# Moving the first LayerNorm of blocks 1 to 3 to earlier steps of a fused attention and feed-forward kernel

## The chip, the cores and the metric

The kernel runs on one core of one Trainium2 chip. The metric is the device time of one execution in microseconds, lower being better.

## The reference, cut to what matters

One adaptive-LayerNorm block: attention over the last 512 cached keys, then a feed-forward part, both with a residual. Shapes: x is 2048 x 512, 32 query heads of 128, 8 key heads.

```python
def _layernorm(x, axis=-1, eps=1e-05):
    m = jnp.mean(x, axis=axis, keepdims=True)
    v = jnp.var(x, axis=axis, keepdims=True)
    return (x - m) / jnp.sqrt(v + eps)
# ... sa, ca, ga, sb, cb, gb are the six 512-wide rows of silu(c) @ w_mod
x = A_x
h = _layernorm(x, axis=-1) * (1 + ca) + sa
x = x + ga * _A_ref(h, A_k_cache, A_v_cache, A_wq, A_wo)     # attention
h = _layernorm(x, axis=-1) * (1 + cb) + sb
x = x + gb * _B_ref(h, B_w1, B_w2)                           # feed-forward
```

There are two LayerNorms per row: "the first" feeds the Q projection, "the second" feeds the feed-forward part.

## The kernel before

The 2048 queries are four blocks of 512. The program is written as 128 steps, one head of one block each (32 steps per block), and a feed-forward tail. In each step TensorE gets scores, the Q projection of a later step, the PV product (softmax weights times values) of the step before, and up to four output-projection matmuls. All other work is a *task* with a step at which it is put into its engine's instruction stream; in the VectorE lines of the prediction, the reciprocal behind a write that stands 3.83 us comes only after it, so a late task holds up what is behind it.

```python
def add_ln(b, which, s0):
    dst, r = (hT[b % 2], R_hT[b % 2]) if which == 1 else h2_of[b]
    for tl in range(TPB):
        add(s0 + tl, lambda t=b * TPB + tl: ln_stat(t))                  # steps s0 .. s0+3
    add(s0 + TPB, lambda: ln_rstd(b))                                    # s0+4
    for tl in range(TPB):
        add(s0 + TPB + 1 + tl // 2, lambda t=b * TPB + tl: ln_norm(t))   # s0+5, s0+6: writes xn
    add(s0 + TPB + 2, ln_dmaT)                                           # s0+6: DMA transpose xn -> xnT
    for cc in range(DC):
        add(s0 + TPB + 5 + cc // 2, lambda cc=cc: ln_mod_sb(cc, dst, r, which))   # s0+9, s0+10: reads xnT
```

There is one `xn` and one `xnT` tile, used by every LayerNorm. `ln_norm` and `ln_mod_sb` (the scale-and-shift that makes hT for Q and h2T for the feed-forward) run on VectorE. VectorE also empties the single buffer in PSUM, the memory that matmuls write into, of the PV product, and the next PV product waits for that:

```python
def pv_mms(u):
    # ... 16 matmuls into o_ps
    kb.op(DVE, lambda e: e.reciprocal(rinv[:, u, :], o_ps[:, :, P]), ...)        # L1511
    kb.op(DVE, lambda e: e.tensor_tensor(o_sb[u % NOS][:, :, :], o_ps[...], rinv[...], op=ALU.mult), ...)   # L1512
    dma(oT[u % NOT][:, :, :], o_sb[u % NOS][:, :, :]..., transpose=True)
```

## Time and profile before

| | before |
|---|---|
| median (first three runs) | 563.0 us (562.78 to 563.45) |
| profiled span | 561.0 us |
| TensorE busy / VectorE busy | 98% / 45% |
| PV beat, with / without output projection | 3.497 / 2.633 us |
| PV intervals off the beat among the first 126 | 8, together 1.33 us too long |

The most useful reading of this kernel is not a busy share but the *beat*: the list of times at which each of the 128 PV products starts, taken from the TensorE timeline. Each interval should be 2.633 or 3.497 us; whatever is longer is time that TensorE lost. The profile lines are in the prediction below.

### The profile page before, as it was taken

To read this page: it belongs to the slowest core of one execution; us is meant where nothing else is said; L and a number is where in the kernel's file an instruction comes from. 1 tells how busy PE (TensorE), PEld (TensorE's weight loads), DVE (VectorE), ACT (ScalarE), POOL (GpSimd) and SP (SyncE) were. 2 spreads that over 40 slices of the span, in tenths; PEclk is the share of its full clock that TensorE was granted. 3 is DMA by queue.
4 is the path that set the end of the run, shared out by engine and by line. 5 is a ranking of instruction groups with operands and counts; after the bars stand their busy time and mean duration, and the time that the engine had idled before them with its cause. 6 is when DMAs were issued, how large, how long until landed. Compare 5 with 4: busy or idle time off the path is not lost.

```text
span 561.0 us, 9655 instructions
## 1 busy us (share of the span) xinstructions
PE 550.8 (98%) x4057; PEld 314.7 (56%) x4132; DVE 252.4 (45%) x550; ACT 350.4 (62%) x453; POOL 51.7 (9%) x46
## 2 busy tenths in 40 slices
PE   7999999999999999999999999999999999999998
PEld 3565555555555555555555555555555654444444
DVE  3455556643336745333347453333354448321134
ACT  5986666666666666666666666666666644432500
POOL 1020002003220000033000000332000000000000
PEclk9999999999999999999999999999999999999999
DMA  9797566512132155242532531121214210210001
GB/s 270 205 206 176 143 164 88 113 39 38 39 76 39 39 90 136 56 96 57 132 57 57 85 63 39 39 38 39 39 39 72 44 30 0 40 37 23 21 29 47
DMA packets 113308, 42.66 MB, mean 76 GB/s; under 512 B 93928, under 2 KB 112104, under 8 KB 113256
## 3 DMA queue, kind: packets, MB, share of 16 engines
q1 hardware_dynamic: 112024, 40.82, 34.5%
q10 hardware_dynamic: 1232, 1.15, 0.6%
q8 instruction: 33, 0.54, 0.4%
q14 instruction: 19, 0.16, 0.1%
HBM read 18.35 MB, written 2.10 MB: 36 GB/s over the span
## 4 chain that ended last, share of the span: by engine, by line
PE 93%; DMA 4%; DVE 2%; issue 1%; DVEq 0%
PE psS L1367 27%; PE psO L1367 26%; PE psQ L1367 22%; PE psW L1367 18%; DMA xnT<-xn 3%; DMA x<-in_A_x_dram 1%; DVE o L1512 0%; DVE st L1377 0%; DVE xn L1388 0%; PE psS L1370 0%; DVE acc L1534 0%; DVE mv L1378 0%; DVE hT L1396 0%; DVE rinv L1511 0%; DVE rstd L1593 0%
## 5 line engine op out<-in xcount | busy, mean ns | idle before, releaser
L1501 ACT ACTIVATE PT<-psS 128x1024 bf16<-128x1024 f32 x256 | 262.7, 1028 | 128.2 <-PE psS L1367 128.2
L1367 PE MATMUL psS<-qT,kT 128*128 128x512 bf16 x510 | 151.4, 379 | 0.1
L1367 PEld LDWEIGHTS psO<-v,PT 128*128 128x128 bf16 x2048 | 126.3, 98 | 31.9 <-DVE o L1512 2.6
L1367 PE MATMUL psO<-v,PT 128*128 128x129 bf16 x2048 | 137.0, 220 | 0.6 <-DVE o L1512 0.6
L1367 PE MATMUL psQ<-hT,wq 128*128 128x512 bf16 x505 | 130.2, 379 | 0.2
L1367 PE MATMUL psW<-wo,oT 128*128 128x512 bf16 x452 | 118.1, 379 | 3.2
L1511 DVE RECIPROCAL rinv<-psO 128x4 f32<-128x4 f32 x128 | 23.3, 182 | 216.0 <-PE psO L1367 216.0
L1512 DVE TENSOR_TENSOR o<-psO,rinv 128x512 bf16<-128x512 f32 x128 | 88.5, 691 | 4.7 <-DVE rinv L1511 0.3
L1367 PEld LDWEIGHTS psQ<-hT,wq 128*128 128x128 bf16 x508 | 49.6, 98 | 60.7 <-issue 0.5
L1367 PEld LDWEIGHTS psS<-qT,kT 128*128 128x128 bf16 x512 | 49.5, 98 | 58.9 <-ACT PT L1501 0.7
L1493 ACT ACTIVATE qT<-psQ 128x512 bf16<-128x512 f32 x127 | 75.3, 593 | 0.5 <-PE psQ L1367 0.5
L1680 ACT ACTIVATE wq<-psS 128x512 bf16<-128x512 f32 x56 | 33.4, 597 | 49.4 <-PE psS L1367 49.4
L1367 PEld LDWEIGHTS psW<-wo,oT 128*128 128x128 bf16 x512 | 44.9, 98 | 32.9 <-DVE acc L1534 1.2
L1534 DVE TENSOR_TENSOR acc<-psW,acc 128x512 f32<-128x512 f32 x48 | 33.1, 690 | 6.7 <-PE psW L1367 6.7
L1367 PE MATMUL psO<-wmw,wq 128*128 128x512 bf16 (+1 forms) x164 | 32.7, 352 | 0.3
L1537 POOL TENSOR_TENSOR acc<-acc,gaf 128x512 f32<-128x512 f32 x12 | 15.2, 1266 | 156.5 <-DVE acc L1534 149.7
L1383 POOL TENSOR_TENSOR rstd<-rstd,cst 128x4 f32<-128x4 f32 x7 | 7.2, 1033 | 213.5 <-DVE rstd L1382 213.5
L1691 DVE TENSOR_TENSOR PT<-psO,gbf 128x512 f32<-128x512 f32 (+1 forms) x12 | 7.5, 624 | 40.4 <-PE psO L1367 40.4
L1367 PE MATMUL psS<-h2T,wmw 128*128 128x512 bf16 x110 | 25.2, 379 | 0.1
L1367 PEld LDWEIGHTS psO<-wmw,wq 128*128 128x128 bf16 x168 | 15.3, 98 | 16.6
L1367 PE MATMUL psS<-hT,wmw 128*128 128x512 bf16 x110 | 24.4, 379 | 0.1
L1377 DVE BATCH_NORM_STATS2 st<-x 128x6 f32<-128x512 bf16 x31 | 21.0, 678 | 4.7 <-DMA x<-in_A_x_dram 4.7
(77 smaller groups left out, 189.4 us busy)
## 6 DMA issues: line engine op xcount, KB each, us to landing
wo<-in_A_wo_dram SPq DMA_DIRECT2D x4, 1024.0 KB, 6.0
wq<-in_A_wq_dram SPq DMA_DIRECT2D x7, 512.0 KB, 5.7
wmw<-in_B_w_dram SPq DMA_DIRECT2D x14, 256.0 KB, 3.1
wmw<-in_w_mod_dram SPq DMA_DIRECT2D x5, 512.0 KB, 4.8
oT<-o SPq DMA_TRANSPOSE x128, 2.4
out_dram<-PT SPq DMA_DIRECT2D x15, 128.0 KB, 1.7
x<-in_A_x_dram SPq DMA_DIRECT2D x3, 512.0 KB, 4.2
v<-in_A_v_cache_dram SPq DMA_DIRECT2D x8, 128.0 KB, 4.2
```

The lines of the kernel that those rows point to most:

```text
L1367: kb.op(PE, lambda e: e.matmul(out_ap, lhsT, rhs, start=start, stop=stop), reads=reads, group_writes=[R_b[k] for k in bk], signal=signal)
L1377: kb.op(DVE, lambda e: e.bn_stats(st[:, t, :], x_sb[:, t, :]), reads=[R_x[t]], writes=[R_st[t]])
L1383: kb.op(POOL, lambda e: e.tensor_tensor(rstd[:, sl], rstd[:, sl], cst[:, 0:1].to_broadcast([P, hi - lo]), op=ALU.pow), reads=R_rstd[sl] + ...
L1493: kb.op(ACT, lambda e: e.activation(qT[u % NQT][:, :], bank[bk], ACTF.Copy), reads=[R_b[bk]], writes=[R_qT[u % NQT]])
L1501: kb.op(ACT, lambda e: e.activation(PT[u % NPT][:, pr * 2:pr * 2 + 2, :], s_ps[pr][:, :, :], ACTF.Exp, scale=scale), reads=[R_b[pr * 2], R ...
L1511: kb.op(DVE, lambda e: e.reciprocal(rinv[:, u, :], o_ps[:, :, P]), reads=[R_b[5], R_b[6]], writes=[R_rinv])
L1512: kb.op(DVE, lambda e: e.tensor_tensor(o_sb[u % NOS][:, :, :], o_ps[:, :, 0:P], rinv[:, u, :].unsqueeze(2).to_broadcast([P, TPB, P]), op=A ...
L1534: kb.op(DVE, lambda e: e.tensor_tensor(acc[:, tl, :], bank[WBK], acc[:, tl, :], op=ALU.add), reads=[R_b[WBK], R_acc[tl]], writes=[R_acc[tl]])
L1537: kb.op(eng, lambda e: e.tensor_tensor(acc[:, tl, :], acc[:, tl, :], gaf[:, :], op=ALU.mult), reads=[R_acc[tl], R_ga], writes=[R_acc[tl]])
L1680: kb.op(ACT, lambda e: e.activation(h1T[b % 2][:, fc, :], bank[bk], ACTF.Relu), reads=[R_b[bk]], writes=[R_h1[b % 2][fc]], pre=all_events( ...
L1691: kb.op(DVE, lambda e: e.tensor_tensor(yt[i][:, c0:c1], bank[bk][:, c0:c1], gbf[:, c0:c1], op=ALU.mult), reads=[R_b[bk], R_gb], writes=[R_ ...
```

## The change

Its effect: the first LayerNorm of a block is never under way in the same steps as the second LayerNorm of another block. The diff moves it nine steps (from 15 to 24 steps ahead of the block), its x load ten, and rearranges the modulation sums and the value-range reductions of the first 38 steps to make room for block 1.

```diff
-            add(max(R * g, 3), lambda g=g, i=i, op=op: kb.op(DVE, lambda e: e.tensor_reduce(vmax...
+            add((3, 5, 12, 16, 20, 24, 28, 32)[g], lambda g=g, i=i, op=op: kb.op(DVE, lambda e: e.tensor_reduce(vmax...
 ...
     for b in range(1, NB):
-        add(H * b - 20, lambda b=b: load_x(b))
-        add_ln(b, 1, H * b - 15)
+        add(H * b - 30, lambda b=b: load_x(b))
+        add_ln(b, 1, H * b - 24)
     for b in range(NB - 1):
         add_ln(b, 2, H * (b + 1) + 19)
 ...
-    for sl, steps in ((2, (5, 6, 7, 9)), (3, (10, 11, 13, 14)), (4, (15, 25, 26, 27)), (5, (29, 30, 31, 33))):
+    for sl, steps in ((2, (6, 7, 15, 19)), (3, (21, 22, 23, 25)), (4, (26, 27, 29, 30)), (5, (31, 33, 34, 35))):
 ...
-    for sl, s in ((2, 10), (3, 27), (4, 38), (5, 105)):
+    for sl, s in ((2, 20), (3, 27), (4, 36), (5, 105)):
```

More of the change, by code (lines that the diff above doesn't have):

```diff
@@ L1634, in build_fast @@
         for i, op in enumerate((ALU.max, ALU.min)):
-            add(max(R * g, 3), lambda g=g, i=i, op=op: kb.op(DVE, lambda e: e.tensor_reduce(vmax[:, i, g:g + 1], v_sb[:, g, :, 0:Dh], axis=AX.XY, op=op),
+            add((3, 5, 12, 16, 20, 24, 28, 32)[g], lambda g=g, i=i, op=op: kb.op(DVE, lambda e: e.tensor_reduce(vmax[:, i, g:g + 1], v_sb[:, g, :, 0:Dh], axis=AX.XY, op=op),
                                                              reads=[R_v[g]], writes=[R_vmax]))
```

## The prediction

> **What bounds the kernel now.** I read the page first, then the waits of all engines, then the timelines of TensorE and VectorE around the places that the waits name.
>
> ```profile
> PE 550.8 (98%) x4057; PEld 314.7 (56%) x4132; DVE 252.4 (45%) x550; ACT 350.4 (62%) x453; POOL 51.7 (9%) x46
> PE   7999999999999999999999999999999999999998
> PE 93%; DMA 4%; DVE 2%; issue 1%; DVEq 0%
> ```
>
> TensorE is the bound from the second slice to the end; nothing else is close. The whole question is therefore how many microseconds TensorE stands still because of the work that the change moves. The kernel runs in 128 steps (one head of one block of 512 queries each), then a feed-forward tail. In a step, TensorE does scores, a Q projection, the PV product and, when there is work, four output-projection matmuls. I listed the start of every PV product from the PE timeline: with output projection the beat is 3.497 us, without it (the first eight intervals and two near the end) 2.633 us, and it repeats to 1 ns in 118 of the first 126 intervals. Only in two places is it off. This is the PE timeline at the first of them:
>
> ```profile
> 202.37 1.07 PE L1367 MATMUL psO<-v,PT 128*128 128x129 bf16 x16
> ...
> 206.33 1.08 PE L1367 MATMUL psO<-v,PT 128*128 128x129 bf16 x16 [0.30 <-DVE o L1512]
> ...
> 209.84 1.07 PE L1367 MATMUL psO<-v,PT 128*128 128x129 bf16 x16
> ...
> 213.51 1.08 PE L1367 MATMUL psO<-v,PT 128*128 128x129 bf16 x16
> ```
>
> The intervals are 3.96, 3.51 and 3.67 us in place of 3.497. PV waits there for the VectorE line that empties the single PSUM buffer of PV (L1512). The VectorE timeline shows why that line was late:
>
> ```profile
> 200.20 0.69 DVE L1512 TENSOR_TENSOR o<-psO,rinv 128x512 bf16<-128x512 f32 x1
> 204.72 0.73 DVE L1388 TENSOR_SCALAR xn<-x,mv,rstd 128x512 bf16<-128x512 bf16 x2 [3.83 <-DMA xnT<-xn]
> 205.37 0.17 DVE L1511 RECIPROCAL rinv<-psO 128x4 f32<-128x4 f32 x1
> ...
> 211.90 0.73 DVE L1396 TENSOR_SCALAR hT<-xnT,modc 128x512 bf16<-128x512 bf16 x2 [3.54 <-DMA xnT<-xn]
> 212.55 0.17 DVE L1511 RECIPROCAL rinv<-psO 128x4 f32<-128x4 f32 x1
> ```
>
> Two LayerNorms are under way at once there: the first one of block 2 and the second one of block 0. They share one xn and one xnT tile. The second LayerNorm cannot write xn until the first one's transposing DMA has read it (VectorE, which runs in order, stands 3.83 us), and then the first one's scale-and-shift waits for another transpose (3.54 us). The same pair of waits comes once more, near 317 and 324 us, for blocks 3 and 1. In the waits view (total us, times, longest us):
>
> ```profile
> DVE hT L1396 <- DMA xnT<-xn: 11.4, 3, 4.2
> DVE xn L1388 <- DMA xnT<-xn: 7.6, 2, 3.8
> ...
> PEld psO L1367 <- DVE o L1512: 2.6, 4, 0.8
> ...
> PE psO L1367 <- DVE o L1512: 0.6, 2, 0.3
> ```
>
> One of the three hT waits lies in the tail and is no business of the change. Four VectorE waits of 3.5 to 3.8 us remain, 14.8 us in all; but TensorE has lost only a small part of that.
>
> There is a second thing in the program's order. Steps of the old plan: first LayerNorm of block 2 in steps 49 to 59, its transpose at 55, its scale-and-shift at 58 and 59; second LayerNorm of block 0 in steps 51 to 61, its transpose at 57. The second transpose is issued before the first LayerNorm's scale-and-shift reads xnT, so hT of block 2 is made from block 0's rows. The trace agrees: the wait that ends at 211.90 is for the transpose issued at 207.54. The kernel before computes the queries of blocks 2 and 3 from the wrong rows; the change looks like the repair of that, and the time is its side effect.
>
> **What the Trainium skill says.** "Perfetto Trace Analysis", section "Optimization Strategy", says to find the gaps on the engine that should be saturated and the semaphore behind each. That is the method here; the gap list above is its result. "TensorE: Matmul & The Clock Gate", section "Back-to-back issue gap", gives 518 cycles at 2.4 GHz for 512 columns, 216 ns: the trace has four such matmuls in 0.86 us on the chain of waits, 215 ns each, so between the gaps TensorE issues without pause and no other saving hides in it. "VectorE: DVE Perf Modes", section "The TRN2 errata", gives (N+151)/0.96 ns for an fp32 tensor_tensor, 691 ns at 512: the group row of L1512 has 691. "DMA: Bandwidth & Descriptors", section "Two DMAs through the same engine are not ordered", says the completion semaphore is the only order that an author has; this is why reuse of xn costs VectorE the whole landing of the transpose, 5.91 us in the chain of waits.
>
> **The change part by part.**
>
> *First LayerNorm of blocks 2 and 3, nine steps earlier* (the diff moves 15 to 24 steps before the block, so they run in steps 40 to 50 and 72 to 82, the second LayerNorms still in 51 to 61 and 83 to 93). No shared tile is wanted by both. What is gained is the sum of the late beats: (3.963 + 3.507 + 3.668 + 3.506) - 4 x 3.497 = 0.66 us at the first place and (3.932 + 3.507 + 3.714 + 3.507) - 4 x 3.497 = 0.67 us at the second: **1.33 us**. Why so little of 14.8: PV's evacuation normally ends about 2.02 us after PV starts (reciprocal 1.11 us after, reciprocal and L1512 0.91 us together), and the next PV comes at 3.50, so VectorE may be 1.48 us late for nothing. At 202.37 the reciprocal came at 205.37 instead of 203.48, 1.89 us late, and PV lost 0.46; 1.89 - 1.48 = 0.41, so the account closes. Elsewhere VectorE had 1.2 to 1.9 us idle in each beat anyway. No instruction is added or taken away.
>
> *First LayerNorm of block 1, steps 17 to 27 to steps 8 to 18.* It costs nothing before (no beat off there). After, its parts fall into a time with less slack: in steps 1 to 8 the beat is 2.63 us, so the evacuation may slip only 0.6 us. The first statistics (about 0.9 us for one tile) come in step 8, where the before kernel has the value maximum and minimum (1.40 us, at 34.69) and still 0.41 us idle; that pair moves to step 12. From step 9 the beat is 3.50. The fullest new step is 12: 1.40 plus 0.16. Nothing gets near 3.50 - 0.91 = 2.6 us of free VectorE. Cost expected 0.
>
> *Loading block 1's x at step 2 instead of 12.* 512 KB more in the busiest stretch of the DMA engines, which is the one real risk:
>
> ```profile
> 24.00:38.00 14.00, 13.89 (x123) 8.84 (x124) 9.47 (x19) 12.98 (x17) 0.00 (x0) 1.00 1.05 218
> 38.00:52.00 14.00, 13.89 (x111) 8.32 (x112) 8.13 (x16) 9.73 (x13) 3.25 (x1) 1.00 0.61 139
> ```
>
> These are windows of 14 us; the last two columns are the DMA engines' share and GB/s. From 24 to 38 us they are full, so what is queued behind the new load should land about 512 KB / 218 GB/s = 2.4 us later (an estimate from this row). What then runs short? x itself: issued at about 23.5 us, wanted by step 8's statistics at 34.7; the slowest landing of an x block in this trace is 6.8 us after issue, so 4 us are left. The Q weights of group 3 landed at 34.87 and are used near 40.2: 3 us left. The output tile ring has four buffers, so the evacuation of unit 8 at 39.35 waits for the transpose of unit 4, which landed at 36.40, later 38.8: 0.5 us left, and another 1.5 us before TensorE would notice. The output projection's second half (heads 4 to 7) starts at 42.4 and its last transpose landed at 39.8; at most 42.2 later. All hold, two of them narrowly. Expected cost about 0.05 us.
>
> *The transpose of block 1's LayerNorm* moves to step 14, about 56 us, among the loads of group 5; before, it took 6.2 us at 86.8. From 56.5 that ends at 62.7, and its reader in step 17 comes at 64.5. Holds.
>
> *Modulation sums (VectorE partial products, GpSimd reductions).* They are rearranged into free steps, same count, 0.48 to 0.77 us each. The gate row is ready in step 20 and a bit, needed near step 35. Expected cost 0. The modulation columns in step 48 (2.8 us on VectorE, at 172.8) now come one step before scale-and-shift of block 2 instead of its statistics; before, the reciprocal slipped to 175.66, about 0.2 us, and no beat was off.
>
> Sum: 563.0 - 1.33 + 0.05 = 561.7 us.
>
> **The rivals.** First, *the early load starves TensorE*: the transposes of outputs, Q weights or x land late enough in 30 to 45 us to stop PV or the output projection. For it: the DMA share of 1.05 and an in-order issue queue in which four output transposes already back up between 30.9 and 38.6 us. Against: the margins above. It would cost 0.5 to 2 us, so the time would be 562.2 to 563.7: no gain. Second, *a new wait takes the old one's place*: the single LayerNorm's own transpose arrives after its reader even without an overlap, as in the tail. Against: the isolated first LayerNorm of block 1 and second LayerNorm of block 2 run in the before trace with every beat at 3.497. It would leave 562.3 or so. Third, *the gain is larger than the stalls seen*, because 14.8 us of VectorE idling vanish. Against: TensorE's beats hold all that counts; VectorE at 45% is not the bound. It would need 550 us, and I give it almost nothing.
>
> **Range and chances.** The most that can come off is 1.33 us, 0.24%, so neither 2% line is in reach by any mechanism I see. Runs of the kernel before spread over 0.7 us. The range covers full gain with a lucky spread (561.1) to almost no gain (562.7). Faster by over 2%: 0.01; within 2%: 0.98; slower: 0.01.
>
> **What would show it.** Right: no wait of xn on the transpose, no wait of hT on it outside the tail, PV beats of 3.497 us from step 50 to 61 and 82 to 93, a span near 559.7. Each landing between 30 and 45 us some 2 us later, without a PV beat off. Wrong: a PV interval above 2.64 in steps 1 to 8 or above 3.50 in 9 to 20, with a DMA as releaser of VectorE or TensorE; or beats as before with other lines in the gaps.

## The result, and the profile after

| | before | after |
|---|---|---|
| median | 562.9 us (562.78 to 563.45, 6 runs) | 561.47 us (561.3 to 561.72, 6 runs) |
| ratio | | 0.9974, 95% interval 0.9961 to 0.9987 |
| profiled span | 561.0 us | 559.8 us |
| PV intervals off the beat (first 126) | 8, 1.33 us | 0 |

Ratios are the mean time of one kernel's runs over that of the other's of the same rounds, so not quite the ratio of the medians. The interval excludes 1, so a small gain is there.

Two lines of the page after, TensorE's and VectorE's busy time and the chain of work that ended last:

```profile
PE 554.5 (99%) x4132; PEld 315.2 (56%) x4132; DVE 252.6 (45%) x550; ACT 350.4 (63%) x453; POOL 52.1 (9%) x46
...
PE 98%; DMA 1%; DVE 1%; issue 0%
```

The DMA part of the chain went from 4% to 1%. The busy time of TensorE must not be compared: it rises by 3.7 us in a shorter run, because 75 matmul records (4132 less 4057) were missing from the trace before; the weight loads are 4132 in both. (The trace of e1 below has no late beat and 4057 records too, and reads 551.0 us.)

The TensorE timeline after, PV products only, at the place that the prediction shows for before (start, duration, instruction, repeats):

```profile
202.48 1.07 PE L1367 MATMUL psO<-v,PT 128*128 128x129 bf16 x16
...
205.98 1.07 PE L1367 MATMUL psO<-v,PT 128*128 128x129 bf16 x16
...
209.47 1.07 PE L1367 MATMUL psO<-v,PT 128*128 128x129 bf16 x16
...
212.97 1.07 PE L1367 MATMUL psO<-v,PT 128*128 128x129 bf16 x16
```

All intervals are 3.50 us. The VectorE timeline there, and then the only line on a transposing wait that is left in the waits view (total us, times, longest):

```profile
203.81 0.69 DVE L1512 TENSOR_TENSOR o<-psO,rinv 128x512 bf16<-128x512 f32 x1
204.45 0.69 DVE L1534 TENSOR_TENSOR acc<-psW,acc 128x512 f32<-128x512 f32 x1
205.06 0.73 DVE L1388 TENSOR_SCALAR xn<-x,mv,rstd 128x512 bf16<-128x512 bf16 x2
207.09 0.18 DVE L1511 RECIPROCAL rinv<-psO 128x4 f32<-128x4 f32 x1 [1.30 <-PE psO L1367]
```

```profile
DVE hT L1396 <- DMA xnT<-xn: 4.2, 1, 4.2
```

The xn write at 205.06 waits for nothing, and the reciprocal has 1.30 us of idle time before it. The one hT wait left is in the tail, as before. The account of the spans: 561.013 - 559.772 = 1.24 us is the 1.33 us of late beats, less 0.11 us by which the first PV started later in this run (17.07 against 16.96 us), plus 0.03 us of tail.

The order of the shared tile can be read too. These are the transposes of xn in the timelines of the issuing queue, before and then after, around the first overlap:

```profile
198.71 1.96 SPq L1300 DMA_TRANSPOSE xnT<-xn  x1
...
207.54 1.64 SPq L1300 DMA_TRANSPOSE xnT<-xn  x1
```

```profile
167.30 1.67 SPq L1300 DMA_TRANSPOSE xnT<-xn  x1
...
205.81 1.63 SPq L1300 DMA_TRANSPOSE xnT<-xn  x1
```

and the reads of xnT for block 2 in VectorE's timeline after:

```profile
177.19 0.72 DVE L1396 TENSOR_SCALAR hT<-xnT,modc 128x512 bf16<-128x512 bf16 x2
...
179.94 0.72 DVE L1396 TENSOR_SCALAR hT<-xnT,modc 128x512 bf16<-128x512 bf16 x2
```

Before, the reads came at 211.90 and 213.97, after the second transpose; after, they come between the two. So before, hT of block 2 was made from block 0's second LayerNorm. Both kernels pass the correctness comparison all the same. A 32-bit evaluation of the reference on a CPU with blocks 2 and 3 fed from the wrong rows in this way differs from the right one by at most 0.0007, where the output's standard deviation is 2.6: the gated attention term itself has a standard deviation of only 0.00015.

### The profile page after: what moved, and what is told of

The parts are those of the page before. It is cut to its first block, busy times and chain, and to the rows that moved or that the text cites. A ratio compares the mean times of both kernels' runs of the same rounds, so it can differ in the third digit from the quotient of the medians.

```text
span 559.8 us, 9728 instructions
## 1 busy us (share of the span) xinstructions
PE 554.5 (99%) x4132; PEld 315.2 (56%) x4132; DVE 252.6 (45%) x550; ACT 350.4 (63%) x453; POOL 52.1 (9%) x46
## 4 chain that ended last, share of the span: by engine, by line
PE 98%; DMA 1%; DVE 1%; issue 0%
PE psS L1367 28%; PE psO L1367 27%; PE psQ L1367 23%; PE psW L1367 20%; DMA x<-in_A_x_dram 1%; DVE st L1377 0%; PE psS L1370 0%; DVE mv L1378 0%; DVE rstd L1593 0%; DVE PT L1691 0%; DVE PT L1693 0%; DVE tmp L1431 0%; DVE sc_bf L1432 0%; DVE tmp L1430 0%
## 5 line engine op out<-in xcount | busy, mean ns | idle before, releaser
L1367 PE MATMUL psW<-wo,oT 128*128 128x512 bf16 x512 | 130.6, 379 | 0.0
```

The costliest lines, as they stand in the source:

```text
L1367: kb.op(PE, lambda e: e.matmul(out_ap, lhsT, rhs, start=start, stop=stop), reads=reads, group_writes=[R_b[k] for k in bk], signal=signal)
```

## The experiments

**Theory:** the two LayerNorms hand the shared tiles xn and xnT over too late; VectorE stands for that, and TensorE loses the part of VectorE's lateness that goes beyond a fixed slack. **Rivals:** the early steps give part of the gain; or VectorE and the transposing queue are simply too crowded when two LayerNorms run in the same steps. Repeated runs of one kernel differ by up to 1.7 us (the kernel before, 562.5 to 564.19 us in one set of nine), and the 95% intervals are about 0.14% (0.8 us) to each side. The profiles show where much of that spread sits: the first PV started between 16.76 and 17.66 us in the profiles, and the tail after the last PV took 106.4 to 106.8 us. The beats repeat to a few ns.

### One part alone, and the rest alone

```diff
# e1_blocks23, against before: only blocks 2 and 3 move
-        add(H * b - 20, lambda b=b: load_x(b))
-        add_ln(b, 1, H * b - 15)
+        add(H * b - (20 if b == 1 else 30), lambda b=b: load_x(b))
+        add_ln(b, 1, H * b - (15 if b == 1 else 24))
```

> One part of the change alone: the first LayerNorm of blocks 2 and 3 (and their x loads) at the new steps, everything else as before. Theory (the shared LayerNorm tiles made VectorE late, and that is the whole gain): all PV beats off the first start go away, 1.33 us less in the beats, median near 561.5 to 561.6, ratio to before 0.9976. Rival (the early steps, i.e. block 1's LayerNorm, the modulation sums and the value ranges, give part of the gain): some gain is missing here, 562.0 or more.

Measured: 561.43 us median against 563.04, ratio 0.9969 (0.9955 to 0.9983). No beat off.

```diff
# e2_rest, against after: blocks 2 and 3 stay where they were
-        add(H * b - 30, lambda b=b: load_x(b))
-        add_ln(b, 1, H * b - 24)
+        add(H * b - (30 if b == 1 else 20), lambda b=b: load_x(b))
+        add_ln(b, 1, H * b - (24 if b == 1 else 15))
```

> The complement: everything of the change except blocks 2 and 3, which stay 15 steps ahead. Theory: the eight late PV intervals stay, about 1.33 us over the beat, median near 562.9, ratio 1.000. Rival (the early steps give part of the gain): below 562.5.

Measured: 563.2 us median, ratio 1.0 (0.9986 to 1.0014). The same eight beats are off, by 1.26 us in all. The two halves of the change are thereby separated: blocks 2 and 3 bring everything, the rearranged first 38 steps bring and cost nothing that can be seen.

### How much distance is needed

```diff
# e3_two_steps, against before
-        add_ln(b, 1, H * b - 15)
+        add_ln(b, 1, H * b - (15 if b == 1 else 17))
# e5_second_later, against before
-        add_ln(b, 2, H * (b + 1) + 19)
+        add_ln(b, 2, H * (b + 1) + 21)
# e4_one_step, against before
-        add_ln(b, 1, H * b - 15)
+        add_ln(b, 1, H * b - (15 if b == 1 else 16))
```

> The kernel before with the first LayerNorm of blocks 2 and 3 moved by two steps only (17 ahead in place of 15). Both LayerNorms are still under way in the same steps (49 to 57), but the first one's scale-and-shift is ordered ahead of the second one's transpose, and the second writes xn in step 56, three steps (10.5 us) after the first one's transpose of about 6 us was issued. Theory (only the hand-over of the shared tiles matters): no beat off, median near 561.5, as the whole change. Rival (two LayerNorms in the same steps overload VectorE): late beats remain, 562.2 to 562.9.

Measured: 561.79 us, ratio 0.9973 (0.996 to 0.9987), no beat off. VectorE's timeline at the place of the first overlap:

```profile
200.89 0.73 DVE L1396 TENSOR_SCALAR hT<-xnT,modc 128x512 bf16<-128x512 bf16 x2
201.53 0.73 DVE L1388 TENSOR_SCALAR xn<-x,mv,rstd 128x512 bf16<-128x512 bf16 x2
...
205.03 0.73 DVE L1396 TENSOR_SCALAR hT<-xnT,modc 128x512 bf16<-128x512 bf16 x2
205.67 0.73 DVE L1388 TENSOR_SCALAR xn<-x,mv,rstd 128x512 bf16<-128x512 bf16 x2
```

The two LayerNorms share the same steps, one directly behind the other, and none of the four lines has a wait. So crowding in these steps does not by itself cost time, and two steps are enough for the whole gain and for the right rows.

> The kernel before with the second LayerNorm of blocks 0 to 2 two steps later in place of the first one earlier. Same distance between the two as in the run with 17 steps. Theory (only the distance counts, not which one moves or the early part of the program): no beat off, near 561.5. Rival (what counts is that the first LayerNorm leaves the steps with the modulation columns or the x additions): late beats remain, 562.2 to 562.9.

Measured: 561.49 us, ratio 0.9971 (0.9958 to 0.9985), no beat off. Which LayerNorm moves does not matter.

> The kernel before with the first LayerNorm of blocks 2 and 3 one step earlier (16 ahead). Theory, from the timeline of before: the first transpose is issued two steps (7 us) before the second LayerNorm writes xn, so the xn wait is gone; but half of the scale-and-shift still comes after the second transpose and waits for it, about 3.5 us of VectorE, which makes PV about 0.3 us late at each of the two places: 0.4 to 0.8 us over the beat in all, against 1.33 with 15 and 0 with 17, median about 562.1. Rival (all or nothing): 1.33 as before, or 0. The rows of half of the columns are still taken from the other block, as in the kernel before, on purpose.

Measured: 561.56 us, ratio 0.9973 (0.9959 to 0.9987), and no beat off at all: the expected 0.4 to 0.8 us did not come. The wait did:

```profile
207.24 0.69 DVE L1512 TENSOR_TENSOR o<-psO,rinv 128x512 bf16<-128x512 f32 x1
210.69 0.73 DVE L1396 TENSOR_SCALAR hT<-xnT,modc 128x512 bf16<-128x512 bf16 x2 [2.76 <-DMA xnT<-xn]
211.34 0.17 DVE L1511 RECIPROCAL rinv<-psO 128x4 f32<-128x4 f32 x1
```

The reciprocal before that one was at 207.02, so the next was due at 207.02 + 3.50 = 210.52 and came 0.82 us late. I had carried over the 3.5 us wait from the kernel before. The transpose itself took as long as there (4.27 us from issue to landing, 4.33 before), but it was issued 0.49 us after the start of a PV product (206.40 against 205.91) in place of 1.21 us (207.54 against 206.33), because the xn wait ahead of it was gone. What is left, 0.82 us, is inside the slack that the doses below measure. This kernel also shows that time and correctness are two thresholds: one step gives the whole time, while half of the columns are still read after the wrong transpose.

### The steps unchanged, but tiles of their own

```diff
# e6_own_tiles, against before (core of it)
+    LN = {1: (xn, R_xn, xnT, R_xnT, "xnT"), 2: (xn2, R_xn2, xnT2, R_xnT2, "xoT")}   # xn2, xnT2 lie in wmw
-    def ln_norm(t):
+    def ln_norm(t, k=1):
+        xn, R_xn = LN[k][:2]
 ... likewise ln_dmaT and ln_mod_sb; k = 2 for the second LayerNorm of blocks 0 and 1
-    for i, s in enumerate([s for s in range(57, NU) if s % HQ in (1, 2, 3, 4)][:FC]):
+    for i, s in enumerate([s for s in range(97, NU) if s % HQ in (1, 2, 3, 4)][:FC]):
```

> The kernel before, steps of both LayerNorms unchanged (15 ahead), but the second LayerNorm of blocks 0 and 1 has xn and xnT tiles of its own, in the part of the weight tile that is free after the start; the feed-forward weights are loaded from step 97 on in place of 57 for that. Theory (the sharing of the two tiles is the cause): no xn or hT wait on a transpose outside the tail, no beat off, near 561.5, and rows from the right block. Rival (it is the crowding of VectorE and of the transposing queue in these steps): late beats remain, at least 0.5 us over the beat.

Measured: 561.67 us, ratio 0.9972 (0.9959 to 0.9986), no beat off, no wait on a transpose outside the tail. Separately allocated tiles did not fit into SBUF (such a kernel does not build), which is why they lie in the weight tile. In VectorE's timeline the second LayerNorm's write (its tile is named wmw here) and the first one's read of its own transpose:

```profile
201.51 0.72 DVE L1393 TENSOR_SCALAR wmw<-x,mv,rstd 128x512 bf16<-128x512 bf16 x2
...
208.50 0.73 DVE L1403 TENSOR_SCALAR hT<-xnT,modc 128x512 bf16<-128x512 bf16 x2
```

With every LayerNorm task in its old step, the stalls vanish when the sharing vanishes. That is the most direct proof of the cause, and with e3 it rules out crowding. (The later weight loads are a second difference of this kernel; e3 and e5 reach the same without it.)

### What lateness costs

```diff
# e7_dose and e10_dose_short_beat, against after
+    for s_, n_ in ((98, 4), (102, 5), (106, 6), (110, 7)):      # e10: ((4, 4), (98, 8))
+        for _ in range(n_):
+            add(s_, lambda: kb.op(DVE, lambda e: e.tensor_reduce(vmax[:, 0, 0:1], v_sb[:, 0, :, 0:Dh], axis=AX.XY, op=ALU.max), ...))
```

> The changed kernel with idle VectorE work added where nothing else is due: 4, 6, 7 and 8 repeated value reductions (about 0.66 us each back to back) in steps 98, 102, 106 and 110. Theory (PV's evacuation may be late by about 1.45 us at no cost): free VectorE time in such a beat is 3.50 - 0.91 = 2.59 us, so the evacuation is late by about 0.05, 1.37, 2.03 and 2.69 us, and PV loses 0, 0, 0.6 and 1.2 us: 1.8 us in all. Rival (TensorE loses every microsecond that VectorE is late): 0.05, 1.4, 2.0 and 2.7 us, 6.1 us in all.

The kernel that ran held 4, 5, 6 and 7 reductions, not the 4, 6, 7 and 8 of the text. It is read by the lateness that the profile shows. One dose in VectorE's timeline, with the reciprocals around it:

```profile
388.96 0.18 DVE L1511 RECIPROCAL rinv<-psO 128x4 f32<-128x4 f32 x1 [1.94 <-PE psO L1367]
...
389.79 5.00 DVE L1658 TENSOR_REDUCE vmax<-v 128x1 f32<-128x512 bf16 x7
394.71 0.17 DVE L1511 RECIPROCAL rinv<-psO 128x4 f32<-128x4 f32 x1
```

The reciprocal was due at 388.96 + 3.50 = 392.46 and came 2.25 us late. Its PV interval in the TensorE timeline was 4.307 us, 0.81 over the beat. With the same reading everywhere:

| where | reciprocal late by, us | PV interval over the beat, us | difference |
|---|---|---|---|
| e7, 4 reductions | 0.08 | 0 | |
| e7, 5 reductions | 0.80 | 0 | |
| e4_one_step, 210.69 | 0.82 | 0 | |
| e7, 6 reductions | 1.52 | 0.09 | 1.43 |
| before, at 211.90 | 1.60 | 0.17 | 1.43 |
| before, at 204.72 | 1.89 | 0.47 | 1.42 |
| e7, 7 reductions | 2.25 | 0.81 | 1.44 |
| e10, 8 reductions | 2.97 | 1.54 | 1.43 |

The difference is the lateness less the loss, left blank where nothing was lost. In these rows TensorE loses the lateness less 1.43 us and never less than nothing. The rival, that it loses every microsecond of lateness, is out.

> The changed kernel with repeated value reductions (0.72 us each back to back, as the run with four doses showed; that run's kernel held 4, 5, 6 and 7 of them, not the 4, 6, 7 and 8 that its text names): 4 in step 4, where the beat is 2.63 us, and 8 in step 98, where it is 3.50. Theory (the free lateness is what TensorE does between two PV products less the evacuation: 1.43 us in the long beat, so 1.43 - 0.86 = 0.57 in the short one): in step 4 the evacuation is late by 4 x 0.72 - (2.63 - 0.91) = 1.16 and PV loses 0.59 us; in step 98 it is late by 8 x 0.72 - 2.59 = 3.17 and PV loses 1.74. Rival (the slack is the same 1.43 in any beat): 0 in step 4, 1.74 in step 98.

Measured, from two PV starts of the long beat in this run's TensorE timeline:

```profile
350.27 1.07 PE L1367 MATMUL psO<-v,PT 128*128 128x129 bf16 x16
...
355.30 1.08 PE L1367 MATMUL psO<-v,PT 128*128 128x129 bf16 x16 [1.37 <-DVE o L1512]
```

The interval is 5.03 us for 2.97 us of lateness (last row of the table). In step 4, with the 2.63 us beat, the reciprocal came 0.95 us late and the interval was 3.10, so 0.47 lost and a slack of 0.48 us (one dose):

```profile
25.44 1.07 PE L1367 MATMUL psO<-v,PT 128*128 128x129 bf16 x16
...
28.54 1.07 PE L1367 MATMUL psO<-v,PT 128*128 128x129 bf16 x16 [0.30 <-DVE o L1512]
```

The slack does shrink with the beat, which the rival denied. Both lateness figures that I had written down were 0.2 us too large, and the short beat's slack came out at 0.48 in place of 0.57. The trace shows where these 0.09 us lie: PV started 0.15 us after the end of the evacuation there (28.54 against 27.70 + 0.69), and 0.06 us after it in the long beat (355.30 against 354.55 + 0.69). Why is open.

### The load that should have delayed the queue

```diff
# e8_x_later, against after
-        add(H * b - 30, lambda b=b: load_x(b))
+        add(H * b - (28 if b == 1 else 30), lambda b=b: load_x(b))
```

> The changed kernel with block 1's x loaded in step 4, right behind the 1 MB of output projection weights, in place of step 2. It is for the step of the prediction that failed: the load delayed what came behind it by 0.1 to 0.2 us after 30 us, not by 2.4. Theory (at step 2 it filled a stretch in which the DMA engines were idle; behind the weights there is none): the Q weights of group 3 and the output transpose behind them land 1.5 to 2.5 us later than in the changed kernel (35.0 and 36.6 us there), and no PV beat is off. Rival (the load is cheap anywhere[...]): they land within 0.5 us of the changed kernel's.

Measured: the Q weights of group 3 landed at 36.64 us against 35.03 in the changed kernel (1.6 later), the next output transpose at 38.79 against 36.55 (2.2 later), and no beat was off (one run, 561.53 us). So an estimate of 2.4 us is of the right size for a load behind the weights, but at step 2 the DMA engines were not full. Three windows of before and the same of after (window, length, then busy time of TensorE, weight loads, VectorE, ScalarE and GpSimd; last: granted clock, DMA share, GB/s):

```profile
17.00:20.00 3.00, 2.95 (x32) 2.06 (x32) 0.88 (x2) 3.00 (x6) 0.00 (x0) 1.00 0.33 100
20.00:24.00 4.00, 3.95 (x40) 2.59 (x39) 2.78 (x6) 3.77 (x6) 0.00 (x0) 1.00 0.75 193
24.00:28.00 4.00, 4.00 (x38) 2.59 (x37) 2.79 (x6) 3.79 (x6) 0.00 (x0) 1.00 0.81 219
```

```profile
17.00:20.00 3.00, 3.00 (x32) 1.98 (x30) 0.87 (x2) 3.00 (x5) 0.00 (x0) 1.00 0.41 124
20.00:24.00 4.00, 4.00 (x42) 2.70 (x40) 2.67 (x6) 3.77 (x6) 0.00 (x0) 1.00 0.69 209
24.00:28.00 4.00, 4.00 (x37) 2.48 (x35) 2.21 (x5) 3.79 (x6) 0.00 (x0) 1.00 1.08 316
```

The x load went into a hole: between 24 and 28 us the share rises from 0.81 to 1.08 and 316 GB/s are moved in place of 219. Behind that stretch both kernels are alike. A delay did exist, but early and briefly: the output transpose right behind the load landed at 26.07 us in place of 24.80 (24.96 in e8, without the load there), the output projection weights issued at 25.62 landed at 31.58 in place of 31.36. The first PV of the changed kernel's run came 0.11 us later as well, so about 0.1 us of that second delay remains.

## Why the prediction was right

Predicted 561.7 us (561.1 to 562.7), measured 561.47. By its own steps:

- *Gain of 1.33 us from blocks 2 and 3.* Right in size and cause. All eight late intervals are gone, with this part alone they are gone (e1), without it they stay (e2), and they go by any means that ends the late hand-over (e3, e5, e6).
- *Slack of 1.48 us.* Right in kind; the runs give 1.43, which is why 1.89 - 1.48 = 0.41 fell short of the 0.47 that PV lost. This is the term that turns 14.8 us of VectorE waits into 1.33 us. Two figures beside it were off: the 0.6 us for the short beat measures 0.48 (e10), and the idle time of VectorE ahead of the reciprocal "elsewhere" is 0.33 to 2.59 us in the beats of 3.50 us in which it was not late, not 1.2 to 1.9.
- *Block 1's LayerNorm into the short beats at no cost.* Right: no beat is off from step 1 on. The transpose was issued at 55.65 and landed at 61.88, its reader came at 65.19.
- *The early x load delays what is behind it by 2.4 us.* Wrong, and with it "each landing between 30 and 45 us some 2 us later". The Q weights landed at 35.03 in place of 34.87, the output transpose at 36.55 in place of 36.40, and 0.11 us of both is the later start of that run. Two terms failed: the issue came at 21.01 us, not 23.5, and I read the DMA share from a 14 us window (1.05), whose first 4 us were at 0.81. The 0.05 us of cost that hung on it did not appear; it was too small to matter for the time.
- *Modulation sums and columns.* Right: the reciprocal behind the columns slipped to 175.78 and no beat is off.
- *The rivals.* The starved TensorE did not come, not even with the load behind the 1 MB of weights (e8). The new wait did not come. A gain beyond the beats did not come: the medians differ by 1.43 us, the beats by 1.33, and the rest is within the spread of start and tail. That the median came within 0.2 us of 561.7 is therefore partly luck; the beats carry the proof.
- *The wrong rows before.* The order of transposes and reads bears it out; the runs cannot show the values, since the comparison passes either way.

None of the experiments points to a version that beats both kernels: the changed kernel has no late PV interval left to take away.

## What to carry to other kernels

List the intervals of one repeated instruction on the engine that bounds the kernel, and count only what exceeds the beat: 14.8 us of another engine's waits were worth 1.33 us, because each lateness is free up to what the bounding engine still has to do before it needs the result. When two phases share a scratch tile, compare the *order* of write, transpose and read in the program, not only the waits: a dependency tracker follows the order it is given, and a wrong order is neither a race nor necessarily a failed test. Two steps of distance, or a second tile, did as much for the time here as nine steps and a rearranged start.

## What the Trainium skill lacked or had wrong

- "Perfetto Trace Analysis", section "Optimization Strategy", tells to find the gaps and their semaphores. It lacks that a wait of a non-bounding engine costs nothing up to a slack, and how to measure it: here 1.43 us in a 3.50 us beat and 0.48 us in a 2.63 us beat.
- The same page, section "Identifying the Most-Contended Engine", calls matmul busy time a bad measure. A further reason, not there: records can be missing. 75 of 4132 matmuls were, so busy time rose from 550.8 to 554.5 us while the span fell by 1.24 us.
- "TensorE: Matmul & The Clock Gate", section "Back-to-back issue gap", gives some 131 ns per matmul of 512 columns as the sustained figure for weight-load and matmul pairs, and 216 ns as the isolated one. In this sustained stream the spacing is 0.86 us for four, 215 ns: the isolated figure, on which the prediction rests, and not the sustained one.
- "DMA: Bandwidth & Descriptors", section "Latency and other measured facts", has bandwidths for transposing DMAs (261 GB/s in one case), which would make 512 KB an estimated 2.0 us. From issue to landing these SBUF-to-SBUF transposes took 4.2 to 6.2 us. What decides within that range is on no page, and these runs leave it open too: with an output transpose issued 1.29 us ahead, one took 5.91 us (issued at 198.71, before) and another 4.31 us (at 430.82, before).
- No page warns that a tile shared by two interleaved phases can be read after the wrong write without any race: the trace shows the read at 211.90 us behind the transpose issued at 207.54.
